# The last stage of a retention + two-MLP kernel, laid out by a table of offsets

## The chip, the cores and the metric

One core of a Trainium2 chip. The metric is the device time of one execution in microseconds (us); the kernel before is run three times and the median counts. A core has five engines with a queue each: TensorE (PE; its weight loads are PEld), VectorE (DVE), ScalarE (ACT), GpSimd (POOL) and SyncE (SP), which here issues the DMAs.

## What is computed

```
ret = scale * (q @ k.T) * Dmat          # 4 x 8 heads, 576 positions, decay per head
x   = (ret @ v) as (2304 tokens, 512)
h   = x @ w_in                          # 512 -> 2048
x2  = (h * clip(h + 3, 0, 6) / 6) @ w_out          # 2048 -> 512
h2  = x2 @ w2_in                        # 512 -> 1024
e   = exp(h2 - max(h2)); sm = e / (sum(e) + 1e-9); solu = h2 * sm
ln  = (solu - mean) / sqrt(var + 1e-6) * g_ln
out = ln @ w2_out                       # 1024 -> 512
```

All of it in fp32: each operand is split into a high and a low word (fp32r), and a product is three matmuls (high x high, high x low, low x high).

## The kernel before, in words

Tokens come in blocks of 512, 512, 512, 512 and 256 (numbers 0 to 4). Retention feeds the first MLP; part B of that MLP (the last ten of its sixteen d_ff tiles, `FB`) runs over the blocks in the order 3, 0, 1, 2, 4 and leaves x2 in DRAM (`x2f`). Part C is the second MLP. It works on pairs of token tiles (2 x 128 tokens), nine pairs, in the block order 2, 3, 0, 1, 4. The last stage is part B of block 4 and part C together, from about 440 us on.

For a pair i of part C:
- `load_x2` brings x2 from DRAM, `forms_x2` (L670) makes sums and differences of its quarters on GpSimd and splits them (L240 on ScalarE, L241 on GpSimd). x2 @ w2_in is done as a 2 x 2 block product with seven products instead of eight (`PRODUCTS`).
- `mm_h2` (L709): seven products of six matmuls, each in a PSUM bank of its own; ScalarE and VectorE add the banks up into u2, u4 and the two rows of h2, with a running maximum (L715, L730 to L741).
- `norm` (L746), for each row r of 128 tokens: exp (L750, ScalarE), h times e (L751, VectorE), square (L756, ScalarE), a few 128 x 1 steps, a power (L760 to L762, GpSimd), normalisation (L764, VectorE).
- `transpose` (L774): the 32-bit result is copied into two 16-bit halves (L780) and each goes through a DMA transpose issued by SP (L781). `split_turned` (L783) puts the halves together again (L771 ScalarE, L772 VectorE) and splits into lt (L240, L241).
- `mm_out` (L793): o of one tile, eight d_ff steps of three matmuls (L802), then a copy (L808) and a store.

`part_c` (L811) writes the order as a generator: four products, then the previous pair's `split_turned`, the next pair's load and forms, an o tile, the other products, the norms and transposes, another o tile; two o tiles and a remainder are left for the end. Only the loads marked in program order keep their place. All other instructions are put in order on each engine by a planner with its own estimates, which is how o, products and x2 matmuls come to alternate in small runs. Part B of block 4 runs by `mlp_by_ff` (L310): for each d_ff tile the h matmuls, and three tiles later its x2 matmuls, while the w2 weights come in one by one (`w2_load`, L604) and part C's first products run beside its end.

The PSUM banks: four single ones (`mm_tile`: h, x2, o) and two pairs of banks (`ps_c`, tag h2: accumulators of block 4's x2, then the products).

Of the kernel before, what the change touches and what calls it, by code (L numbers as in the profile page):

```python
# [21 lines left out]
NP = DM // 128  # L22
# [26 lines left out]
W2_FORMS = tuple(w for _, w in PRODUCTS)  # L49
LN_EPS = 1e-6  # L50
# [10 lines left out]

@with_exitstack
def retention_hardswish_solu_kernel(ctx, tc, kt, qt, kn, vt, w1, w2i, w2o, gln, decay, place, out):
# [3 lines left out]
    ve, se, ge = nc.vector, nc.scalar, nc.gpsimd  # L67
# [175 lines left out]
    def mlp_h(t, ff, g, slot):  # L243
# [18 lines left out]
        pool, tag, bufs = slot(ff)  # L262
        g[ff] = pool.tile([128, 2, n], F32R, tag=tag, bufs=bufs, name=f"g{t}_{ff}")
# [321 lines left out]
    def load_x2p(t, k):  # L585
        n = BLOCKS[t][1]
        if k * 512 < NP * n:
# [3 lines left out]
            nc.sync.dma_start(out=part, in_=x2s[t][:, k * share:(k + 1) * share])  # L591
# [3 lines left out]
    def evac_full(t, d, xp):  # L595
# [6 lines left out]
        nc.sync.dma_start(out=x2f[t][:, d], in_=e)  # L602

    def w2_load(f, home):  # L604
        for i in range(2):
            if home == "x4":
                w = [p0.tile([128, 2, 256], F32R, tag="x4", bufs=NP, name=f"w2{f}_{i}_{a}") for a in range(2)]
                w2t[f, i] = [a.rearrange("p a n -> p (a n)") for a in w]
                for a in range(2):
                    nc.sync.dma_start(out=f32(w2t[f, i][a]), in_=w2s[f, i][:, a])  # L610
            else:
                w = w_half(home, i, f"w2{f}_{i}")
                w2t[f, i] = [w[:, a] for a in range(2)]
                nc.sync.dma_start(out=f32(w), in_=w2s[f, i])
# [299 lines left out]
```

## Time and profile before

| | us |
|---|---|
| median of three executions (lowest, highest) | 707.6 (705.43, 711.11) |
| the profiled execution: its own time | 709.63 |
| its span, first to last instruction | 707.5 |
| TensorE busy in the span | 667.5 (94%) |
| VectorE, ScalarE, GpSimd busy | 324.7, 358.2, 315.5 |
| mean granted TensorE clock | 0.983 of 2.4 GHz |

The profiled execution is one execution: its span is what the rows measure, and its own time has what lies around the span. Busy time of TensorE counts pipelined matmuls, so that a busy share near 100% says only that it never stood still.

### The profile page before, as it was taken

What the parts mean: (1) busy time and instruction counts of PE and PEld (TensorE: products, weight loads), DVE (VectorE), ACT (ScalarE), POOL (GpSimd) and SP (SyncE); (2) the same over time, 40 slices, a digit from 0 to 9 for tenths busy, and PEclk for the clock granted to TensorE, in tenths of its full rate; (3) what the DMA queues carried; (4) which work ended last, traced back from release to release, by engine and by line L of the source; (5) the groups of instructions that cost most, each with busy time, mean ns of one, the idle gap of its engine ahead of it and who ended that gap; (6) DMA issues with size and microseconds to landing.
All of it is one profiled execution on the core that took longest, in us unless ns stands there. A gap on an engine that the chain in (4) does not pass through costs nothing.

```text
span 707.5 us, 10683 instructions
## 1 busy us (share of the span) xinstructions
PE 667.5 (94%) x3914; PEld 547.9 (77%) x3914; DVE 324.7 (46%) x606; ACT 358.2 (51%) x651; POOL 315.5 (45%) x342
## 2 busy tenths in 40 slices
PE   9999999999999999999999999985899888899967
PEld 6788888878889888888888888973667667777756
DVE  2555535163206351444743541115756666566660
ACT  6788746265427561553642640523535644555352
POOL 5676733023404241360430430756658756854242
PEclk9999999999999999999999999999899999899998
DMA  9989534295043525678547324994441344033531
GB/s 327 301 286 323 199 105 177 68 302 212 0 143 97 159 79 172 186 246 303 194 155 249 103 112 126 356 334 143 89 104 55 90 110 71 34 76 89 90 74 45
DMA packets 80296, 112.92 MB, mean 160 GB/s; under 512 B 42738, under 2 KB 48114, under 8 KB 80244
## 3 DMA queue, kind: packets, MB, share of 16 engines
q1 hardware_dynamic: 80096, 112.22, 50.6%
q8 instruction: 31, 0.51, 0.3%
q14 instruction: 21, 0.17, 0.1%
q10 hardware_dynamic: 148, 0.01, 0.0%
HBM read 70.80 MB, written 31.98 MB: 145 GB/s over the span
## 4 chain that ended last, share of the span: by engine, by line
PE 70%; POOL 7%; DVE 7%; DMA 6%; issue 6%; ACT 3%; SPq 0%; ACTq 0%; POOLq 0%; DVEq 0%
PE h L250 25%; PE x L271 17%; PE acc L271 9%; PE o L802 7%; PE h L724 5%; PE xp L373 3%; DMA lhT<-lh 3%; PE s L373 2%; POOL s L680 2%; POOL lt L241 2%; DVE h L751 2%; PE u L373 1%; DMA wraw<-in_w_dram 1%; DVE lh L780 1%; DMA rq<-in_qt_dram 1%
## 5 line engine op out<-in xcount | busy, mean ns | idle before, releaser
L265 POOL TENSOR_TENSOR g<-gf,g 128x512 fp32r<-128x512 f32 (+1 forms) x80 | 97.3, 1217 | 208.9 <-ACT g L264 197.6
L271 PE MATMUL x<-g,w 128*128 128x512 f32 x576 | 132.5, 389 | 0.5 <-DVE gf L261 0.4
L250 PE MATMUL h<-xb,w 128*128 128x512 f32 (+1 forms) x600 | 132.8, 359 | 0.1
L271 PEld LDWEIGHTS x<-g,w 128*128 128x128 f32 x576 | 108.0, 188 | 23.7 <-DVE gf L261 0.8
L802 PE MATMUL o<-w,lt 128*128 128x512 f32 (+1 forms) x456 | 109.0, 391 | 7.5 <-ACT lt L240 7.3
L261 DVE SCALAR_TENSOR_TENSOR gf<-r,h 128x512 f32<-128x512 f32 (+1 forms) x80 | 50.5, 632 | 139.7 <-ACT r L260 110.3
L250 PEld LDWEIGHTS h<-xb,w 128*128 128x128 f32 x600 | 100.1, 189 | 16.1 <-ACT x2p L346 0.5
L802 PEld LDWEIGHTS o<-w,lt 128*128 128x128 f32 x456 | 84.9, 195 | 28.0 <-ACT lt L240 9.4
L250 PE MATMUL h<-xB,w 128*128 128x512 f32 x360 | 82.4, 389 | 0.0
L271 PE MATMUL acc<-g,w 128*128 128x512 f32 (+1 forms) x384 | 79.9, 336 | 0.0
L250 PEld LDWEIGHTS h<-xB,w 128*128 128x128 f32 x360 | 67.6, 188 | 14.0
L260 ACT ACTIVATE r<-h,half 128x512 f32<-128x512 f32 (+1 forms) x80 | 50.9, 638 | 52.0 <-PE h L250 52.0
L271 PEld LDWEIGHTS acc<-g,w 128*128 128x128 f32 x384 | 63.3, 189 | 9.1
L264 ACT ACTIVATE g<-gf 128x512 fp32r<-128x512 f32 (+1 forms) x80 | 46.9, 586 | 44.8 <-DVE gf L261 43.2
L241 POOL TENSOR_TENSOR lt<-lT,lt 128x512 fp32r<-128x512 f32 x36 | 52.5, 1481 | 31.2 <-ACT lt L240 31.1
L724 PE MATMUL h<-w2t,xs 128*128 128x512 f32 x162 | 43.5, 407 | 9.7 <-DVE u L734 6.6
L131 DVE TENSOR_SCALAR wz<-wz 128x512 int32<-128x512 int32 x44 | 28.6, 650 | 40.1 <-ACT wz L123 40.0
L724 PEld LDWEIGHTS h<-w2t,xs 128*128 128x128 f32 x162 | 30.5, 195 | 19.2 <-DVE u L734 9.4
L771 ACT ACTIVATE lT<-lhT 128x1024 uint16<-128x1024 uint16 x18 | 24.6, 1368 | 36.2 <-DMA lhT<-lh 36.0
L123 ACT ACTIVATE wz<-wraw 128x512 f32<-128x512 f32 x44 | 29.0, 659 | 17.7 <-DMA wraw<-in_w2o_dram 8.9
L241 POOL TENSOR_TENSOR xb<-xa,xb 128x512 fp32r<-128x512 f32 (+7 forms) x32 | 27.5, 879 | 22.9 <-ACT xb L240 22.9
L715 DVE CUSTOM_DVE_ANT_0 h<-h,u 128x512 f32<-128x512 f32 x36 | 24.7, 685 | 25.1 <-PE h L724 18.3
(119 smaller groups left out, 863.5 us busy)
## 6 DMA issues: line engine op xcount, KB each, us to landing
wraw<-in_w_dram SPq DMA_DIRECT2D x32, 512.0 KB, 4.8
xs<-xb SPq DMA_DIRECT2D x12, 512.0 KB, 5.7
xB<-xs SPq DMA_DIRECT2D x12, 512.0 KB, 6.6
rv<-in_vt_dram SPq DMA_DIRECT2D x16, 288.0 KB, 5.3
x2l<-x2s SPq DMA_DIRECT2D x18, 256.0 KB, 4.2
out_dram<-osb SPq DMA_DIRECT2D x17, 256.0 KB, 2.1
x2s<-x2p SPq DMA_DIRECT2D x16, 256.0 KB, 2.7
x2f<-x2o SPq DMA_DIRECT2D x16, 256.0 KB, 3.6
```

Source lines behind the costliest of these rows:

```text
L123: first = se.activation(out=z.bitcast(F32), in_=raw[:, :, 1].bitcast(F32), func=ACTF.Prelu, scale=2.0 ** -112, alpha=2.0 ** 32)
L131: ve.tensor_scalar(out=z, in0=z, scalar1=3, scalar2=None, op0=ALU.logical_shift_left)
L241: ge.tensor_tensor(out=x[:, 1, c], in0=src, in1=f32(x[:, 0, c]), op=ALU.subtract)
L250: nc.tensor.matmul(hp, w1t[ff, 0][:, a, c], xb[t, p][:, b, :n], start=(p == 0 and i == 0), stop=(p == NP - 1 and i == 2),)
L260: se.activation(out=r, in_=hp, func=ACTF.Relu, scale=1.0 / 6.0, bias=half)
L261: ve.scalar_tensor_tensor(out=gf, in0=r, scalar=1.0, in1=hp, op0=ALU.min, op1=ALU.mult)
L264: se.activation(out=g[ff][:, 0], in_=gf, func=ACTF.Copy)
L265: ge.tensor_tensor(out=g[ff][:, 1], in0=gf, in1=f32(g[ff][:, 0]), op=ALU.subtract)
L271: nc.tensor.matmul(acc, w1t[ff, 1][:, a, c], g[:, b], start=(first and i == 0), stop=(last and i == 2))
L373: keep(nc.tensor.matmul(*args, **kw))
L724: nc.tensor.matmul(acc, x2w[i][x][k][a], w2t[w, k][b], start=(k == 0 and n == 0), stop=(k == 1 and n == 2),)
L802: nc.tensor.matmul(op, lt[:, a, ff % 4], w[b][:, c0:c0 + n], start=(ff == 0 and j == 0), stop=(ff == NFF2 - 1 and j == 2),)
```

## The change

Only the last stage is changed. Every instruction of it, on each of the five queues, is now kept in program order (`Pinned`), and the program order comes from a list of (time, step) pairs, sorted. The times are offsets in microseconds from the planned ends of the seven products of each pair, e[0] to e[6]; only their order is used. What the table lays out:

- Block 4's h for all ten d_ff tiles comes first (`mlp_hs`, still ordered by the planner), with its g kept in SBUF; its x2 follows as 40 units of three matmuls, by d_ff tile, in two single banks.
- The products run in groups of two, two, two and one (`GROUPS`), each group of two in one pair of banks. Between the groups stand fillers: five units of x2 in pair 0, four in pair 1, four units of o (three matmuls each) in pairs 2 to 7, none in pair 8. The rest of o follows.
- u2 and u4 live in the halves of row 1's h2, the weights of t4 in the tags r and gf, x2 in one load of 512 KB in other tags, the split forms in eight fixed tiles.
- `half_out`, `half_in`, `split_hi` and `split_lo` are the old `transpose` and `split_turned` in single steps, placed one by one.
- `STEPS_B` gets an entry of its own for each block.

The diff, cut to its core:

```diff
-STEPS_B = (6, 20, 42, 50, 58, 66)
+STEPS_B = ((6, 20, 42, 50, 58, 66), (6, 20, 42, 50, 58, 66), (6, 20, 42, 50))
-C_AHEAD = 8
+GROUPS = ((0, 1), (2, 3), (4, 5), (6,))
+UNIT, SMALL = 0.68, 0.36
+class Pinned:
+    def __init__(self, tc, engine):
+        self.keep, self.engine = tc.keep_in_program_order, engine
+    def __getattr__(self, name):
+        op = getattr(self.engine, name)
+        return lambda *args, **kw: self.keep(op(*args, **kw))
...
-        return pb.tile([128, 2, 512], F32R, tag="wb", bufs=8, name=name)
+        return pb.tile([128, 2, 512], F32R, tag="wbi" if i == 0 else "wbo", bufs=4, name=name)
...
-            x2r[i] = [p0.tile([128, 2, 256], F32, tag=tag, bufs=2, name=f"x2r{i}_{tag}") for tag in ("r", "gf")]
-        for k in range(2):
-            nc.sync.dma_start(out=x2r[i][k], in_=x2f[t][:, 2 * k:2 * k + 2, 256 * c:256 * c + 256])
+            raw = raw_bufs[i % 2]
+        x2r[i] = raw[:, :2], raw[:, 2:]
+        sy.dma_start(out=raw, in_=x2f[t][:, :, 256 * c:256 * c + 256])
...
+    def product(i, p):
+        if p % 2 == 0:
+            ab = ps_c.tile([128, 2, 512], F32, tag="h2", bufs=2, name=f"h2_{i}_{p}")
+            banks[i, p], banks[i, p + 1] = ab[:, 0], ab[:, 1]
...
-    def part_c():
...
+    load_x2(0)
+    load_x2(1)
...
+    to_load = {18: ("b11", "wbi"), 22: ("b21", "wbi"), 28: ("t2", "wi"), 36: ("t1", "wi")}
+    for i, _ in enumerate(mlp_hs(t, FB, g4, g_4)):
+        if i == 6:
+            for step in chain(*forms_x2(0)):
+                step()
+        if i in to_load:
+            w2_load(*to_load[i])
+    ve, se, ge, te, sy = (Pinned(tc, e) for e in (ve, se, ge, te, sy))
+    for f, home in (("b22", "wi"), ("t3", "x4"), ("t4", "r")):
+        w2_load(f, home)
...
+    fill(4, 0)
+    for i in range(last + 1):
+        starts.append(now)
+        for group in GROUPS:
+            for p in group:
+                at(now, product, i, p)
+                now += 2 * UNIT
+                ends[i, p] = now
+            fill(5 if i == 0 else 4, 4 if 2 <= i < last else 0)
+    fill(0, out_left)
...
+    for i in range(last + 1):
+        e = [ends[i, p] for p in range(7)]
+        for when, fn, *args in (
+            (e[0] + 0.2, first_u), (e[1] + 0.6, total, 0, 0, 2, 1), (e[2] + 0.1, add_u, 2, 2),
+            (e[3] + 0.1, add_u, 4, 3), (e[4] + 0.1, total, 0, 1, 4, 4), (e[4] + 0.8, top, 0), (e[4] + 1.0, exp, 0),
+            (e[5] + 0.1, total, 1, 1, 4, 5), (e[5] + 0.8, add_u, 2, 5), (e[4] + 2.9, weigh, 0),
+            (e[4] + 4.4, small, 0), (e[4] + 4.5, square, 0), (e[4] + 5.8, power, 0),
+            (e[6] + 0.1, total, 1, 0, 2, 6), (e[6] + 0.8, top, 1), (e[6] + 1.0, exp, 1),
+            (e[4] + 7.1, norm, 0), (e[6] + 2.4, weigh, 1), (e[6] + 4.0, small, 1), (e[6] + 4.0, square, 1),
+            (e[4] + 9.2, half_out, 0, 0), (e[4] + 9.9, half_out, 0, 1),
+            (e[6] + 5.3, power, 1), (e[6] + 6.7, norm, 1), (e[6] + 7.6, half_out, 1, 0), (e[6] + 8.3, half_out, 1, 1),
+            (e[4] + 15.3, half_in, 0, 0), (e[4] + 15.4, half_in, 0, 1),
+            (e[4] + 16.8, split_hi, 0, 0), (e[4] + 17.4, split_hi, 0, 1),
+            (e[4] + 17.5, split_lo, 0, 0), (e[4] + 18.8, split_lo, 0, 1),
+            (e[6] + 14.0, half_in, 1, 0), (e[6] + 14.1, half_in, 1, 1),
+            (e[6] + 23.5, split_hi, 1, 0), (e[6] + 24.1, split_hi, 1, 1),
+            (e[6] + 24.2, split_lo, 1, 0), (e[6] + 25.5, split_lo, 1, 1),
+        ):
+            at(when, fn, i, *args)
+        if i + 2 <= last:
+            at(starts[i] + 13.0, load_x2, i + 2)
+        if i < last:
+            spread(i + 1, starts[i], (0.0, 0.8, 3.6, 4.4, 3.6, 4.2, 4.8, 5.5, 5.2, 6.0, 7.3, 8.6))
+    for _, _, fn, args in sorted(events, key=lambda v: v[:2]):
+        fn(*args)
```

## Rows read from the trace of the kernel before

**Rows 1.** The page: busy time of TensorE, and its busy tenths in 40 slices.

```profile
PE 667.5 (94%) x3914; PEld 547.9 (77%) x3914; DVE 324.7 (46%) x606; ACT 358.2 (51%) x651; POOL 315.5 (45%) x342
PE   9999999999999999999999999985899888899967
```

**Rows 2.** Stretches: length, busy PE, PEld, DVE, ACT, POOL (instructions), PEclk, DMA, GB/s.

```profile
440.75:473.80 33.05, 33.05 (x259) 32.08 (x257) 4.90 (x11) 12.34 (x27) 21.01 (x25) 1.00 0.90 326
...
473.80:507.40 33.60, 19.95 (x63) 14.46 (x63) 20.79 (x43) 12.09 (x21) 19.13 (x22) 0.85 0.55 165
...
524.10:548.30 24.20, 23.19 (x96) 17.63 (x96) 15.76 (x33) 12.87 (x22) 16.72 (x18) 1.00 0.41 95
...
524.10:621.00 96.90, 87.49 (x353) 67.27 (x354) 61.49 (x127) 51.12 (x84) 66.20 (x72) 0.96 0.36 82
...
673.80:707.50 33.70, 24.65 (x119) 20.20 (x117) 11.48 (x24) 13.07 (x21) 10.45 (x13) 0.90 0.26 63
```

**Rows 3.** Chain of waits, 400 to 707.5: start, us, what.

```profile
413.71 27.20 PE x L271 x120
...
440.91 5.51 PE h L250 x46
...
603.71 2.93 PE h L724 x6
...
655.13 1.36 PE h L724 x6
...
691.30 12.88 PE o L802 x70
```

**Rows 4.** TensorE's waits, 415 to 707.5: total us, times, longest.

```profile
PE o L802 <- ACT lt L240: 7.3, 3, 5.6
PE h L724 <- DVE u L734: 6.6, 4, 3.5
PE h L724 <- DVE x2o L599: 4.4, 1, 4.4
...
PE h L724 <- DVE u L736: 3.1, 4, 0.8
```

**Rows 5.** Start of the stage: a stretch, GpSimd and VectorE in time, a load.

```profile
450.00:460.00 10.00, 10.00 (x85) 10.00 (x84) 1.26 (x3) 5.37 (x13) 9.92 (x12) 1.00 1.03 413
...
449.46 1.44 POOL L680 TENSOR_TENSOR s<-x2r 128x256 f32<-128x256 f32 x2 [1.87 <-DMA x2r<-x2f]
...
456.31 0.42 DVE L261 SCALAR_TENSOR_TENSOR gf<-r,h 128x256 f32<-128x256 f32 x1 [4.59 <-POOL xs L241]
...
x2r_gf<-x2f SPq DMA_DIRECT2D x3, 256.0 KB, 7.0
```

**Rows 6.** Lines from 520 to 690: duration ns min/median/max, first and last start.

```profile
L751 DVE SCALAR_TENSOR_TENSOR h<-h,e x14: 1208/2056/2294, 535.5 to 679.5; 128x1024 f32<-128x1024 f32 x14
...
L764 DVE TENSOR_SCALAR e<-h,stat x16: 808/812/1362, 520.2 to 683.8; 128x1024 f32<-128x1024 f32 x16
...
L715 DVE CUSTOM_DVE_ANT_0 h<-h,u x28: 664/690/693, 523.4 to 675.3; 128x512 f32<-128x512 f32 x28
...
L772 DVE COPY lT<-lhT x16: 741/748/1845, 528.2 to 689.2; 128x1024 uint16<-128x1024 uint16 x16
...
L750 ACT ACTIVATE e<-h,stat x14: 1135/1144/1160, 534.2 to 678.2; 128x1024 f32<-128x1024 f32 x14
...
L241 POOL TENSOR_TENSOR lt<-lT,lt x29: 1267/1297/2279, 530.9 to 690.0; 128x512 fp32r<-128x512 f32 x29
...
L680 POOL TENSOR_TENSOR s<-x2r_r x4: 730/738/747, 541.3 to 614.1; 128x256 f32<-128x256 f32 x4
...
L762 POOL TENSOR_TENSOR stat<-stat,mhalf x16: 541/732/1377, 519.6 to 682.7; 128x1 f32<-128x1 f32 x16
```

**Rows 7.** Transposes of lhT, 510 to 700: issue on SP (ns), landing.

```profile
L781 SPq DMA_TRANSPOSE lhT<-lh x32: 1237/1288/1397, 522.9 to 687.2; - x32
...
DMA to landing us min/median/max: 3.1/3.3/4.5
```

More of the change, by code (lines that the diff above doesn't have):

```diff
@@ L270, in mlp_x2 @@
         for i, (a, b) in enumerate(((0, 0), (1, 0), (0, 1))):
-            nc.tensor.matmul(acc, w1t[ff, 1][:, a, c], g[:, b], start=(first and i == 0), stop=(last and i == 2))
+            te.matmul(acc, w1t[ff, 1][:, a, c], g[:, b], start=(first and i == 0), stop=(last and i == 2))
     def mlp_hs(t, ffs, g, slot, keep_x=False):
@@ L746, in norm @@
-    def norm(i, r):
-        h, st = h2[i][r], stats[i][r]
+        return sums, his, los
+    def product(i, p):
+        if p % 2 == 0:
+            ab = ps_c.tile([128, 2, 512], F32, tag="h2", bufs=2, name=f"h2_{i}_{p}")
+            banks[i, p], banks[i, p + 1] = ab[:, 0], ab[:, 1]
+        x, w = PRODUCTS[p]
+        for k in range(2):
+            for n, (a, b) in enumerate(((0, 0), (0, 1), (1, 0))):
+                te.matmul(
+                    banks[i, p], x2w[i][x][k][a], w2t[w, k][b], start=(k == 0 and n == 0), stop=(k == 1 and n == 2),
+                )
@@ new lines, in row, with total @@
+    def row(i, r):
+        if (i, r) not in h2:
+            h2[i, r] = p0.tile([128, 2, 512], F32, tag="g", bufs=FA, name=f"h2_{i}_{r}")
+            stats[i, r] = pb.tile([128, 16], F32, tag="stat", bufs=6, name=f"stat{i}_{r}")
+        return h2[i, r], stats[i, r]
+    def total(i, r, m, u, p):
+        h, st = row(i, r)
+        ve.tensor_tensor_reduce(
+            out=h[:, m], in0=banks[i, p], in1=us[i, u], scale=1.0, scalar=MIN, op0=ALU.add, op1=ALU.max,
+            accum_out=st[:, m:m + 1],
+        )
@@ L793, in mm_out @@
     def mm_out(i):
-        r = tiles[i]
         n = DM // 2 if i == len(tiles) - 1 else DM
@@ new lines, in retention_hardswish_solu_kernel, with at, fill @@
+    events = []
+    def at(when, fn, *args):
+        events.append((when, len(events), fn, args))
+    now = 0.0
+    x2_4 = x2_units()
+    outs = chain(*(mm_out(i) for i in range(len(tiles))))
+    small_left, out_left = NP * len(FB), NFF2 * len(tiles) + NFF2
+    starts, ends = [], {}
+    def fill(n_small, n_out):
+        nonlocal now, small_left, out_left
+        for gen, n, length in ((x2_4, min(n_small, small_left), SMALL), (outs, min(n_out, out_left), UNIT)):
+            for _ in range(n):
+                at(now, next, gen, None)
+                now += length
+        small_left -= min(n_small, small_left)
+        out_left -= min(n_out, out_left)
@@ new lines, in retention_hardswish_solu_kernel, with spread, step @@
+    fill(4, 0)
[8 more added lines that the diff above has]
+    fill(0, out_left)
+    def spread(i, n, offsets):
+        made = {}
+        for k, offset in enumerate(offsets):
+            def step(k=k):
+                if not made:
+                    made[0] = list(chain(*forms_x2(i)))
+                made[0][k]()
+            at(n + offset, step)
```

270 lines of the change are left out of this document (124 added, 146 removed).

## The prediction

> **What bounds the kernel now.** I read the page first: TensorE has work in 94% of the span, and its slices are full up to about 475 us and ragged from there on [rows 1]. The reader should see that the ragged part is the last stage, the only one the change lays out anew. The table of stretches puts numbers on it [rows 2]: from 440.75 to 473.8 TensorE is always busy; from 473.8 to 507.4 it has 20 us of work in 33.6, at a mean granted clock of 0.85; then four repeats in 96.9 us, one per pair of token tiles, the first of 24.2; and from 673.8, the end of the last product, to the end of the span 24.7 of 33.7.
>
> How much of it is work? The chain of waits shows the pace: 120 matmuls of 512 columns in 27.20 us, or 0.2267 each, and 46 of 256 columns in 5.51, or 0.1198 each [rows 3]. By the loops the stage has, for the last block, 120 h and 120 x2 matmuls of 256 columns (28.75 us); 9 pairs x 7 products x 6 matmuls = 378 (85.7); and 18 o tiles x 24, of which the last is cut in halves: 408 of 512 columns (92.5) and 48 of 256 (5.75). In sum 212.7 us. It took from 440.75 to 704.2, where the last o ends (691.30 + 12.88), so 263.4. **50.7 us are loss.** TensorE's waits list 32.0 of them in seven rows, from 7.3 to 3.1 [rows 4]: 7.3 on lt, and 24.7 in the other six on something of VectorE or ScalarE that frees a PSUM bank (u, stat, x2o). The other 19 are the pipeline that drains and fills around each stop, and stretches at half of the 2.4 GHz: six matmuls in 2.93 us against 1.36 [rows 3]. From the clocks of [rows 2], 19.95 x 0.15 + 87.5 x 0.04 + 24.65 x 0.10, that is about 9 us.
>
> No other engine is full. Over the four repeats VectorE is busy 61.5 of 96.9 us, ScalarE 51.1, GpSimd 66.2 [rows 2], so 15.4, 12.8 and 16.6 us for a pair. A pair of TensorE alone (42 products, 48 o matmuls) is 90 x 0.2267 = 20.4.
>
> **The change, part by part.** *Arithmetic:* no matmul is added or removed. Per pair the vector work is the same list: seven bank evacuations, two rows of softmax and normalisation, four copies and four transposes out, four copies in, splits. x2 comes by one 512 KB load instead of two of 256 KB. I put these at nothing. The third entry of STEPS_B loses two steps that have nothing left to do (6 + 6 + 4 = 16, the number of halves), and the two names for the "wb" tiles split one pool of 8 into 4 + 4: nothing.
>
> *Last block's h first:* 120 x 0.1198 = 14.4 us, so to 455.15; then 4 x2 units (0.36 each) to 456.6. What has to be there then: xb and weights are resident, b11 may load as soon as two h's are done. All transfers up to the third x2 load are about 10.8 MB (six 1 MB forms and one more, one w_out form, 1.8 MB of x2 in and out); at 326 GB/s, the mean of this stretch before [rows 2], 33 us from 442.5 or to 475; at the 413 GB/s of its best ten microseconds [rows 5], to 468.7. The order is that of use, and the last form (t4) is wanted at 470, by which 9.2 MB are wanted, 22 to 28 us after 442.5: 465 to 471. So transfers are nearly hidden. GpSimd is tighter: the forms of pair 0 start when x2 lands (449.46 before, and the store that it waits for doesn't move) and are about 7.6 us of work beside one g split per h; before, gf on VectorE waits for GpSimd's xs there [rows 5]. With h's packed closer, two gf buffers and four banks let TensorE run six h's ahead; I take **3 us** of stall here, from 0 (all in time) to 8 (all of GpSimd's 7.6 first).
>
> *Products in groups of two, filler between:* two banks each, and the banks of a group are asked for again only a filler, a group and a filler later: 8.2 us with o between, 5.6 with x2 units. The releases (0.7 each) come 1 to 3 us after the group by the table. This is what takes away the 24.7 us on u, stat and x2o. By the table pair 0 lasts 9.52 + 20 x 0.36 = 16.7, pair 1 15.3, pairs 2 to 7 9.52 + 16 x 0.68 = 20.4 each, pair 8 9.52, and what is left of o 33.0 (40 units of 0.68 and 16 of 0.36): 456.6 + 16.7 + 15.3 + 122.4 + 9.5 + 33.0 = 653.5, and 3.3 for the last eviction and store as now (704.2 to 707.5): **a floor of 656.8.**
>
> *Everything pinned:* each engine now stands in the table's order, and behind a late instruction all of that engine waits. So I walked one middle pair with the rows' durations. VectorE's loop goes from the total of product 4 to the same of the next pair [rows 6]: total 0.77 with its read-out, top 0.21, exp on ScalarE 1.33 with its read-out, weigh 1.2 to 2.1 and 0.2, square 1.33, power on GpSimd 1.1 (0.73 and two small ones), norm 0.81, weigh of row 1 2.1 and 0.2: 9.2 to 10.1. Then row 1: two copies and row 1's small steps 1.7 (beside square on ScalarE), the next total 1.2 later behind first_u, norm 0.8, a copy 0.7, so 4.4; its transposes, issued at 1.29 each, land 3.3 us (3.1 to 4.5) after [rows 7], and half_in takes 0.75: 8.4 to 9.6. With 0.1 for each of ten hand-overs the loop is 18.6 to 20.7 us, and up to 21.5 where half_in on ScalarE (1.4) delays the next exp, against TensorE's 20.4. So it is about as long as what should cover it: queued behind half_in on VectorE are the next pair's totals, and TensorE waits for these only when they are 5 us late. Pair 0 and 1, with short fillers, give about 4 us of that lateness away (a loop of 19 to 20 in pair 1, of 15.3). o has more room: lt of pair i is ready 11 us ahead of its use by the table. I take **3 us** for the six pairs (0 if the loop is 19 to 20; 6 x 1.1 = 7 at 21.5).
>
> *The end:* pair 8 has nothing between its groups; the copy that frees the first bank pair comes behind row 1 of pair 7, and I take **1 us** (0 to 2). Row 1's lt must be there 27.2 us after the last product; before, the first split of the last pair was there at 691.3, 17.5 us after it [rows 3], but now there are two osb's and the transposes of pair 7 ahead of it: **2 us** (0 to 5). SP's queue: four transposes, two stores and a load a pair, about 6.5 of 20.4 us. Half clock after such stops: **1**.
>
> Two engines get denser. weigh takes 1.21 us at the least and 2.06 in the middle, GpSimd's split of lt 1.27 at the least and 2.28 at the most [rows 6]. The terms above have the contended value for one weigh in two.
>
> The Trainium skill (SBUF — State Buffer, section SBUF: two separate sides) says that VectorE operations with two SBUF inputs, or in a two-port mode, and GpSimd operations hold one shared port in turn, each for the whole instruction. The stretched values of both engines agree with that [rows 6]; what it would make of this change is the first rival.
>
> **Rivals.** *A. The port or the loop becomes the bound.* From the least values [rows 6], GpSimd needs 7 x 1.27 + 0.73 + 4 x 0.73 + 2 x 0.9 = 14.3 us a pair by itself (splits, xa, sums, power); weigh, norm and half_in of two rows (2.4 + 1.6 + 1.5), if each shuts it out, make 19.8 of 20.4, where it is 19.8 of 24.2 now. For: the stretched rows. Against: total is never stretched (0.66 to 0.69), and the table leaves GpSimd without work for 5 us a pair while weigh of row 0 runs. If only 88% of a period can be filled, it is 22.6, 2.2 x 6 pairs = 13 us more than the floor less 1 us of room: 667 + 12 = **679**.
>
> *B. The start stays late.* The forms, the x2 loads and row 0's first trip meet at 456 to 490, and pairs 0 and 1 have only 14.4 us of x2 to fill with. For: 7.0 us for a 256 KB load in this stretch [rows 5]. Price: x2 of pair 2 six us late, and lt of pair 0 (4 us of room) five late: 667 + 11 = **678**.
>
> *C. Slower: the fixed order ties the engines into one chain.* VectorE stands at half_in of row 1 until its transposes land, and the next pair's totals with it. If the way from half_out to half_in were 12 us instead of 4 to 5 (transposes behind 512 KB loads on the queues), the loop would be 28 us: 8 x 7.6 - 4 = 57 above the floor, so **714**; it decides from a period of 27.2 on, 6.8 above 20.4. Against: the longest landing seen is 4.5 us [rows 7].
>
> *D. No change:* the planner already placed o between products, and what it lost is not order but latency. Against: [rows 4] names banks, which the groups relieve. About **705**.
>
> **The numbers.** 656.8 + 3 + 3 + 1 + 2 + 1 = 666.8 of span. The profiled execution has 2.1 us beside its span and lies 2.0 above the median, so **667**. Chances: this forecast 0.62 (its own range, from the terms' ends, 657 to 680, the sum of the upper ends being 23), A 0.22, B 0.09, C 0.04, D 0.03. The range of 657 to 683 takes in A and B with some of their spread. About 1% is what a measurement of this kernel can tell. Faster by over 1%: 0.94; within 1%: 0.03; slower: 0.03.
>
> **What would show it.** Right: TensorE's waits after 440 fall from 32 to about 8; repeats of 20.4 to 21 us from 490 to 610; clock 1.00 there; last product near 628. Start: a TensorE gap near 455 on gf or x2 forms. A: repeats of 22 to 23 with waits on totals, GpSimd's splits near 1.7 on the mean. C: repeats above 27, VectorE waiting for transposes. Wrong if TensorE runs without gaps and still ends after 680, or if stages before 440 move.

## The result, and the profile after

| | before | after |
|---|---|---|
| median (lowest to highest), us | 709.36 (705.43 to 711.22) | 678.45 (677.07 to 678.76) |
| ratio, 95% interval | | 0.9568 (0.9519 to 0.9616) |
| profiled execution, its span | 709.63, 707.5 | 678.33, 676.5 |
| granted clock, mean | 0.983 | 0.995 |

The kernel became 31 us faster. 667 was predicted, with 657 to 683 around it: the direction and its cause were right, and the forecast was 11 us too low. Of these, 9.7 us lie in the span. The other 1.7 come from the step from span to time: the median of before was taken to lie 2.0 us below its profiled execution, but with a fourth execution (711.22) it lies 0.3 below, and the changed kernel's median lies at its profiled execution. All instructions that the table places have one line in the new profile, L69 (that of `Pinned`), so its rows are read by tile. L260, L271 and L283 are the old L250, L261 and L271.

TensorE's waits from 415 us on, the view of [rows 4] (us in total, times, longest):

```profile
PE h L69 <- DVE stat L69: 4.4, 1, 4.4
PE h L69 <- DVE h L69: 2.9, 5, 1.0
PE o L69 <- DMA w<-w2s: 1.6, 2, 1.2
PE h L260 <- DVE gf L271: 1.0, 1, 1.0
PE x L69 <- DVE gf L271: 0.9, 1, 0.9
```

10.8 us in five rows instead of 32.0 in seven. The stage by stretches, columns as in [rows 2]: h and block 4's first x2 up to the first product; pair 2; pair 6; pair 8; what is left of o, and the end.

```profile
442.13:460.34 18.21, 16.34 (x133) 15.93 (x132) 4.49 (x10) 9.31 (x23) 11.63 (x15) 1.00 0.89 332
492.50:515.09 22.59, 21.00 (x92) 16.75 (x91) 19.80 (x36) 13.35 (x21) 20.93 (x20) 1.00 0.75 195
579.85:601.37 21.52, 20.99 (x91) 16.73 (x90) 19.22 (x32) 12.88 (x21) 18.64 (x19) 1.00 0.43 105
622.91:639.89 16.98, 12.55 (x44) 9.66 (x42) 13.15 (x28) 6.99 (x11) 6.31 (x9) 0.80 0.38 78
639.89:676.50 36.61, 33.13 (x169) 28.23 (x167) 13.53 (x26) 16.33 (x26) 14.56 (x14) 1.00 0.28 73
```

The span that was predicted is 666.8, the measured one 676.5. The difference, term by term:

| part | predicted | measured | difference |
|---|---|---|---|
| stage begins (first h) | 440.75 | 442.13 | +1.4 |
| first h to first product: 15.85 of work, and stall | 3 | 2.36 | -0.6 |
| pairs 0 and 1 | 32.0 | 32.2 | +0.2 |
| pairs 2 to 7, 122.4 of work, and stall | 3 | 8.0 | +5.0 |
| pair 8, 9.52 of work, and stall | 1 | 7.5 | +6.5 |
| rest of o, 33.0 of work, and stall | 2 | 0.1 | -1.9 |
| half clock after stops | 1 | counted in pair 8 | -1.0 |
| last eviction and store | 3.3 | 3.5 | +0.2 |

Two terms carry it: the middle pairs and pair 8. The 1.4 us ahead of the stage are hardly work of the change: up to there TensorE and VectorE have the same instructions in the same order, the other engines differ only by one x2 form and two DMA issues from 434.9 us on, and the first h of the runs below lies anywhere from 439.6 to 443.0. They are therefore compared from the first product on; in the changed kernel it is 216.2 us from there to the end of the span (460.34 to 676.5).

**Pair 8.** TensorE in time, and the total that frees the banks on VectorE (start, us, what, in brackets the wait before it):

```profile
622.91 2.89 PE L69 MATMUL h<-w2b,xt 128*128 128x512 f32 x12
625.63 2.92 PE L69 MATMUL h<-w2t,xt 128*128 128x512 f32 x12
632.99 2.93 PE L69 MATMUL h<-w2b,xt 128*128 128x512 f32 x6 [4.43 <-DVE stat L69]
635.71 4.34 PE L69 MATMUL h<-w2t,xt 128*128 128x512 f32 x12
639.89 2.45 PE L69 MATMUL o<-w,lt 128*128 128x512 f32 x10
...
632.25 0.68 DVE L69 CUSTOM_DVE_ANT_0 h<-h,h 128x512 f32<-128x512 f32 x1
```

Two groups run, and the third wants banks that the first total of this pair still holds. Then six matmuls take 2.93 us and twelve 4.34, against 1.36 [rows 3] and 2.72. That is another 3.2 us, lost to the clock: the granted clock is 0.80 on the mean of this pair, with its stop of 4.43 us, and 1.00 in the pairs ahead of it.

**The middle pairs.** From pair 3 on TensorE stops for no more than 1.0 us at a time, and yet a pair lasts 21.5, not 20.4. So I follow one turn of the vector engines' loop, from one `weigh` of row 0 to the next (start, us, what):

```profile
579.14 2.31 DVE L69 SCALAR_TENSOR_TENSOR h<-h,e 128x1024 f32<-128x1024 f32 x1 [0.39 <-ACT e L69]
...
583.98 1.22 DVE L69 TENSOR_SCALAR e<-h,stat 128x1024 f32<-128x1024 f32 x1 [1.35 <-POOL stat L69]
...
585.12 1.76 DVE L69 SCALAR_TENSOR_TENSOR h<-h,e 128x1024 f32<-128x1024 f32 x1
585.76 3.97 POOL L69 TENSOR_TENSOR lt<-lT,lt 128x512 fp32r<-128x512 f32 x2
...
586.99 1.59 DVE L69 COPY lh<-e 128x1024 uint16<-128x1024 uint16 x1
587.17 1.15 ACT L69 ACTIVATE e<-h,stat 128x1024 f32<-128x1024 f32 x1 [1.53 <-DVE stat L69]
...
588.62 1.66 DVE L69 COPY lh<-e 128x1024 uint16<-128x1024 uint16 x1
...
589.69 0.91 POOL L69 TENSOR_TENSOR stat<-stat 128x1 f32<-128x1 f32 x2
...
591.26 1.22 DVE L69 TENSOR_SCALAR e<-h,stat 128x1024 f32<-128x1024 f32 x1 [0.38 <-POOL stat L69]
...
595.30 1.25 DVE L69 COPY lT<-lhT 128x1024 uint16<-128x1024 uint16 x1
...
596.66 1.15 ACT L69 ACTIVATE lt<-lT 128x512 fp32r<-128x512 f32 x2 [1.65 <-DVE lT L69]
...
598.15 0.67 DVE L69 CUSTOM_DVE_ANT_0 h<-h,h 128x512 f32<-128x512 f32 x1
...
599.43 1.15 ACT L69 ACTIVATE e<-h,stat 128x1024 f32<-128x1024 f32 x1
...
600.70 2.28 DVE L69 SCALAR_TENSOR_TENSOR h<-h,e 128x1024 f32<-128x1024 f32 x1 [0.40 <-ACT e L69]
```

Read it as one chain over three engines that each keep their order. `weigh` of row 0 (579.14), its square on ScalarE, its power on GpSimd, norm (583.98), `weigh` of row 1 (585.12), its square (ready at 588.4). Row 1's power should come now, but GpSimd is in two splits of lt until 589.69. So norm of row 1 comes at 591.26, then two copies, half_in (595.30), and ScalarE's split that waits for it; behind that stand half_in of row 1 and the next exp (599.43), and behind that the next `weigh`: 21.56 us after the last one.

Some of this chain is stretched. VectorE's forms from 536.77 to 622.91, after (busy us, mean ns | idle before):

```profile
L69 DVE COPY lh<-e 128x1024 uint16<-128x1024 uint16 x16 | 22.0, 1395 | 0.1
...
L69 DVE CUSTOM_DVE_ANT_0 h<-h,h 128x512 f32<-128x512 f32 x16 | 10.9, 678 | 0.0
L69 DVE COPY lT<-lhT 128x1024 uint16<-128x1024 uint16 x8 | 9.9, 1242 | 0.0
L69 DVE TENSOR_SCALAR e<-h,stat 128x1024 f32<-128x1024 f32 x8 | 9.8, 1221 | 6.9 <-POOL stat L69 6.9
```

and the same copy before, over four pairs:

```profile
L780 DVE COPY lh<-e 128x1024 uint16<-128x1024 uint16 x18 | 11.6, 689 | 0.1
```

The copy out takes 1.40 us instead of 0.69, half_in 1.24 and norm 1.22 where [rows 6] have medians of 0.75 and 0.81; the total is not stretched (0.68). VectorE is busy 19.2 of 21.5 us where it was 15.4 a pair. So both are in the chain: VectorE itself waits only 0.38 us for row 1's power (591.26), since its stretched copies fill nearly all of that time.

### The profile page after: what moved, and what is told of

It is laid out like the page before. It is cut to its first block, busy times and chain, and to the rows that moved or that the text cites. A ratio compares the mean times of both kernels' runs of the same rounds, so it can differ in the third digit from the quotient of the medians.

```text
span 676.5 us, 10633 instructions
## 1 busy us (share of the span) xinstructions
PE 657.2 (97%) x3914; PEld 545.0 (81%) x3914; DVE 350.2 (52%) x606; ACT 357.2 (53%) x651; POOL 329.8 (49%) x342
## 4 chain that ended last, share of the span: by engine, by line
PE 65%; DVE 10%; POOL 7%; DMA 7%; ACT 6%; issue 4%; SPq 0%; ACTq 0%; POOLq 0%; DVEq 0%
PE h L260 25%; PE x L283 17%; PE acc L283 8%; PE o L69 5%; PE h L69 3%; DVE h L69 3%; PE xp L385 3%; POOL lt L69 2%; DVE lh L69 2%; ACT e L69 2%; DMA wraw<-in_w_dram 2%; POOL stat L69 2%; PE s L385 1%; PE x L69 1%; DVE e L69 1%
## 5 line engine op out<-in xcount | busy, mean ns | idle before, releaser
L283 PE MATMUL x<-g,w 128*128 128x512 f32 x576 | 132.4, 389 | 0.1
L260 PE MATMUL h<-xb,w 128*128 128x512 f32 (+1 forms) x600 | 129.5, 359 | 1.0 <-DVE gf L271 1.0
L283 PEld LDWEIGHTS x<-g,w 128*128 128x128 f32 x576 | 108.0, 188 | 23.3 <-POOL g L277 0.5
L271 DVE SCALAR_TENSOR_TENSOR gf<-r,h 128x512 f32<-128x512 f32 (+1 forms) x80 | 50.6, 633 | 130.9 <-ACT r L270 105.5
L260 PEld LDWEIGHTS h<-xb,w 128*128 128x128 f32 x600 | 98.6, 189 | 17.1 <-DVE gf L271 1.2
L69 PE MATMUL o<-w,lt 128*128 128x512 f32 (+1 forms) x456 | 102.9, 378 | 1.6 <-DMA w<-w2s 1.6
L69 PEld LDWEIGHTS o<-w,lt 128*128 128x128 f32 x456 | 82.3, 188 | 18.4 <-DMA w<-w2s 2.4
L260 PE MATMUL h<-xB,w 128*128 128x512 f32 x360 | 82.4, 389 | 0.0
L260 PEld LDWEIGHTS h<-xB,w 128*128 128x128 f32 x360 | 67.6, 188 | 14.0
L69 POOL TENSOR_TENSOR lt<-lT,lt 128x512 fp32r<-128x512 f32 x36 | 58.4, 1639 | 22.6 <-ACT lt L69 12.2
L69 ACT ACTIVATE e<-h,stat 128x1024 f32<-128x1024 f32 x36 | 41.2, 1145 | 39.4 <-DVE stat L69 39.4
L283 PE MATMUL acc<-g,w 128*128 128x512 f32 (+1 forms) x264 | 61.8, 360 | 0.0
L69 PE MATMUL h<-w2t,xt 128*128 128x512 f32 x216 | 55.5, 401 | 2.9 <-DVE h L69 2.9
L283 PEld LDWEIGHTS acc<-g,w 128*128 128x128 f32 x264 | 46.9, 188 | 8.7
L69 PEld LDWEIGHTS h<-w2t,xt 128*128 128x128 f32 x216 | 41.0, 193 | 13.6 <-DVE h L69 5.0
L69 PE MATMUL h<-w2b,xt 128*128 128x512 f32 x162 | 41.7, 403 | 4.6 <-DVE stat L69 4.4
L69 DVE COPY lh<-e 128x1024 uint16<-128x1024 uint16 x36 | 42.8, 1211 | 0.2
L69 PEld LDWEIGHTS h<-w2b,xt 128*128 128x128 f32 x162 | 30.5, 193 | 12.7 <-DVE stat L69 6.7
```

Source lines behind the costliest of these rows:

```text
L69: return lambda *args, **kw: self.keep(op(*args, **kw))
L260: nc.tensor.matmul(hp, w1t[ff, 0][:, a, c], xb[t, p][:, b, :n], start=(p == 0 and i == 0), stop=(p == NP - 1 and i == 2),)
L271: ve.scalar_tensor_tensor(out=gf, in0=r, scalar=1.0, in1=hp, op0=ALU.min, op1=ALU.mult)
L283: te.matmul(acc, w1t[ff, 1][:, a, c], g[:, b], start=(first and i == 0), stop=(last and i == 2))
```

## The experiments

Four questions: which part of the change gave the 31 us; what holds pair 8; what sets 21.5; and whether the mended versions add up. Times without an interval are of one execution.

### What gave the gain: unpinned, x2_half, groups43

*unpinned*: everything else stays, but the engines are not pinned, so that the planner orders the new stage.

```diff
-    ve, se, ge, te, sy = (Pinned(tc, e) for e in (ve, se, ge, te, sy))
```

> The same list of steps in the same program order, but nothing of the last stage is kept in program order: the planner orders each engine by its own estimates. Theory 'the fixed order is part of the gain': the planner interleaves as before, TensorE's waits on banks come back to 10 us or more, span 685 to 700. Rival 'grouping, filler and program order are the gain and pinning adds little': span 673 to 680.

Measured 690.62 (span 688.6). TensorE's waits, same view and stretch as above:

```profile
PE h L733 <- DVE stat L745: 6.6, 3, 2.3
PE h L733 <- DVE h L756: 6.1, 3, 3.4
PE o L836 <- POOL lt L826: 3.7, 3, 2.1
PE o L836 <- ACT lt L821: 2.5, 2, 1.9
```

18.9 us of stops, 12.7 of them on the totals and additions that free banks. The span lies in the range of the theory, 685 to 700. Against 678.45 the fixed order is worth about 12 us; the rest of the change gives the other 18 or 19, even where the planner orders it. The parts of that rest were not all taken apart: the two runs that follow spoil the filler and the groups, one at a time.

*x2_half*: 16 of block 4's x2 units go ahead of the first product instead of between the products of pairs 0 and 1.

```diff
-    fill(4, 0)
+    fill(20, 0)
...
-            fill(5 if i == 0 else 4, 4 if 2 <= i < last else 0)
+            fill(3 if i == 0 else 2, 4 if 2 <= i < last else 0)
...
-            at(starts[i] + 13.0, load_x2, i + 2)
+            at(starts[i] + (11.0 if i == 1 else 13.0), load_x2, i + 2)
```

> Half of block 4's x2 units (20 of 40) run before the first product, so that pairs 0 and 1 have 12 and 8 units as filler instead of 20 and 16. Work is the same. Theory 'x2 is the cover of the first pairs' chains': what is missing, 7.2 us of cover, comes back as waits of products on banks and of the first o units on lt in pairs 0 to 3; the way from the first h to the start of pair 4 grows by 4 to 7 us, span 680 to 684. Rival 'lateness saturates anyway': the lateness that pairs 0 and 1 give away is lost at pair 8 only once, and the span is within 2 us of 676.5.

Measured 682.93 (span 681.2). From the first h to the end 239.4 us, against 234.4: of the 5.8 us of matmuls that were moved ahead (16 x 0.36; the 7.2 of the expectation counts 20 units), 5.0 are lost. The stops that come back, on TensorE:

```profile
495.50 4.40 PE L69 MATMUL h<-w2b,xt 128*128 128x512 f32 x12 [2.69 <-DVE h L69]
...
502.43 3.68 PE L69 MATMUL o<-w,lt 128*128 128x512 f32 x10 [1.88 <-POOL lt L69]
```

The middle pairs end at the same 21.53. So filler is worth nearly its own time here: the first `weigh` comes 32.5 us after the first h in the changed kernel and 37.2 here, so the vector loop starts 4.7 us later.

*groups43*: groups of four and three products with fillers twice as long.

```diff
-GROUPS = ((0, 1), (2, 3), (4, 5), (6,))
+GROUPS = ((0, 1, 2, 3), (4, 5, 6))
...
-            fill(5 if i == 0 else 4, 4 if 2 <= i < last else 0)
+            fill(10 if i == 0 else 8, 8 if 2 <= i < last else 0)
```

> The products in groups of four and three with twice the filler behind each, instead of 2, 2, 2, 1. Same work. Theory 'the distance from a group to its next use of the banks is what took away the waits': the second group asks at once for the banks of products 0 to 2, and the next pair's first group for those of 4 to 6; before the second group there are 5.4 us of filler and none between the first two bank pairs, so waits on totals come back, 1 to 3 us a pair, span 683 to 700. Rival 'it is the amount of filler in a pair, wherever it stands': span 675 to 679.

Measured 684.27 (span 682.5, just under the theory's 683 and well above the rival's 679), 222.2 us from the first product: 6 more.

```profile
PE h L69 <- DVE stat L69: 12.2, 6, 5.0
```

The waits on the total's banks go from 4.4 us in one to 12.2 in six. That two banks and a filler lie between two uses is what holds TensorE free of VectorE, as the prediction had it.

### What holds pair 8: fill8

In pair 8 o units stand between the groups too, and row 1's last splits come 6 us earlier in the table.

```diff
-            fill(5 if i == 0 else 4, 4 if 2 <= i < last else 0)
+            fill(5 if i == 0 else 4, 4 if 2 <= i <= last else 0)
...
-            (e[6] + 23.5, split_hi, 1, 0), (e[6] + 24.1, split_hi, 1, 1),
-            (e[6] + 24.2, split_lo, 1, 0), (e[6] + 25.5, split_lo, 1, 1),
+            (e[6] + 23.5 - (6.0 if i == last else 0.0), split_hi, 1, 0), ...
```

> Pair 8 gets four o units behind each of its four groups too (and row 1's last splits stand 6 us earlier in the list, so that the shorter remainder of o finds them). Theory 'lateness comes due': VectorE is some 5 us late from pair 3 on; with o between groups the banks are asked for 8.2 us later and little of that shows, in pair 8 they are asked for at once and all of it shows (4.4 us of wait and a stretch at half clock, 17.0 us instead of 9.5). Then pair 8 lasts about 21.5, its wait falls below 1 us, the remainder of o lasts 22 us plus at most 2 of wait for the last lt, and the span is 669 to 672, the time 0.988 to 0.993 of the changed kernel's. Rival 'the end is a chain': what ends last is the way from the last product to the last lt, some 25 us; then o waits 5 us or more for lt in the remainder and the span stays at 675 to 678.

Measured 676.75 (673.28 to 677.35), ratio 0.9532 (0.9502 to 0.9562); in the profiled execution 213.1 us from the first product. The interval overlaps the changed kernel's (0.9519 to 0.9616): by the medians the time is 0.9975 of it, where 0.988 to 0.993 was expected. The profiled execution is the fastest of the four, and what follows is read from it alone. The stop of 4.43 is gone, but one comes that was not there, in the last row's o:

```profile
655.92 0.73 PE L69 MATMUL o<-w,lt 128*128 128x512 f32 x2 [2.20 <-ACT lt L69]
657.27 3.06 PE L69 MATMUL o<-w,lt 128*128 128x512 f32 x12 [0.62 <-POOL lt L69]
```

From the `weigh` of row 0 of pair 8 to the end are 30.1 us instead of 34.6, but that `weigh` stands 1.4 later after the first product (183.0 against 181.6): 3.1 of the 7.5 us come back in this execution, and 1.7 by the medians. The 1.4 come from pair 3, where nothing was edited: a stop of 1.79 us there is followed by matmuls at a granted clock of 0.76 (531 to 538), and the pair lasts 24.1 us instead of 21.7. The stop in pair 8 was a matter of bank room. What is left of o is now 10.9 us shorter, and o waits for the last row's lt. What the earlier splits alone do was not tried.

### What sets 21.5: act_out, skip_lo, power_first

*act_out*: the second of the two copies in `half_out` goes from VectorE to ScalarE.

```diff
-        ve.tensor_copy(out=part, in_=words[:, w])
+        if w:
+            se.activation(out=part, in_=words[:, w], func=ACTF.Copy)
+        else:
+            ve.tensor_copy(out=part, in_=words[:, w])
```

> The second of each row's two 16-bit copies out (half_out, w = 1) goes from VectorE to ScalarE. Theory 'VectorE is the bound, stretched by GpSimd' (busy 19.2 of a 21.5 us period): VectorE falls to about 16.5 us a pair, ScalarE rises from 12.9 to 15.6, the period falls to TensorE's 20.4 to 20.7, pair 8 loses 2 to 4 us of its stall, span 665 to 670. Rival 'a chain of hand-overs through four engines and the transposes is the loop, whoever does the copy': ScalarE's copy takes 1.37 on the same way, the period stays 21.3 to 21.7 and the span 675 to 678.

Measured 672.17 (671.5 to 673.24), ratio 0.9481 (0.9457 to 0.9504), an interval wholly below the changed kernel's; 209.4 us from the first product. VectorE is busy 15.9 of 21 us, GpSimd as before:

```profile
555.00:576.00 21.00, 20.94 (x93) 17.03 (x92) 15.93 (x33) 15.15 (x24) 18.12 (x19) 1.00 0.43 104
```

*skip_lo*: three of the four GpSimd splits of each x2 are left out from pair 2 on. The kernel leaves work out, so its time is a probe and not a gain.

```diff
-            lambda a=a, b=b, v=v: ge.tensor_tensor(...) for a, b, v in splits
+            lambda a=a, b=b, v=v: ge.tensor_tensor(...) for a, b, v in splits[:1 if i >= 2 else 4]
...
-                made[0][k]()
+                if k < len(made[0]):
+                    made[0][k]()
```

> Leaves work out: from pair 2 on the low words of three of the four split x2 forms are not computed (three 128 x 512 subtractions on GpSimd a pair; old values stay). Theory 'GpSimd stretches VectorE': GpSimd falls from 19.2 to some 14 us a pair, VectorE's copies out fall from 1.40 to 1.0 us or less and its busy time from 19.2 to 17 or less, the period to 20.4 to 20.7, span 664 to 669. Rival 'chain of hand-overs': the subtractions left out are not on the chain, so the period stays 21.3 to 21.7 and the span 674 to 678.

Measured 669.34 (span 667.6); 209.0 us. GpSimd is busy 14.0 us in a pair instead of 18.6, and VectorE still 18.35:

```profile
574.29:594.96 20.67, 20.67 (x92) 16.71 (x91) 18.35 (x32) 13.15 (x21) 14.02 (x15) 1.00 0.44 105
...
594.91 1.23 DVE L69 SCALAR_TENSOR_TENSOR h<-h,e 128x1024 f32<-128x1024 f32 x1
```

That the copies would become short was wrong: their mean stays at 1395 ns, and the two splits of lt that stand beside them are still there. `weigh` falls from 2.01 to 1.46: that of row 0, which has no split beside it any more, takes 1.23 us (594.91) and not 2.28.

*power_first*: only GpSimd's order changes. Row 1's two splits of lt go behind the next pair's power, and no instruction is added or removed.

```diff
-            (e[6] + 24.2, split_lo, 1, 0), (e[6] + 25.5, split_lo, 1, 1),
+            (e[6] + 26.2, split_lo, 1, 0), (e[6] + 26.9, split_lo, 1, 1),
```

> Only GpSimd's order changes: row 1's two splits of lt (3.5 to 4 us in the middle pairs, while weigh and the copies out of VectorE run) stand behind the power of the next row instead of ahead of it; no work is added or removed. Theory 'the two engines stretch each other where the table sets them side by side': weigh of row 1 (1.76) and the copies of row 0 (1.6 each) come down, power of row 1 no longer waits behind a split, VectorE's busy time falls from 19.2 to 18 or less, period 20.4 to 20.9, span 668 to 672. Rival 'total work of both engines on the port is what counts, wherever it stands': the splits collide with later VectorE work instead, period 21.3 to 21.8, span 675 to 678.

Measured 671.2 (span 669.4); 210.9 us. The same place of the loop as above, on all engines:

```profile
581.25 1.76 DVE L69 SCALAR_TENSOR_TENSOR h<-h,e 128x1024 f32<-128x1024 f32 x1
...
583.13 0.68 DVE L69 COPY lh<-e 128x1024 uint16<-128x1024 uint16 x1
...
583.85 0.68 DVE L69 COPY lh<-e 128x1024 uint16<-128x1024 uint16 x1
584.01 0.87 POOL L69 TENSOR_TENSOR stat<-stat 128x1 f32<-128x1 f32 x2 [2.08 <-DVE stat L69]
...
585.68 1.64 DVE L69 TENSOR_SCALAR e<-h,stat 128x1024 f32<-128x1024 f32 x1
587.36 2.81 DVE L69 COPY lh<-e 128x1024 uint16<-128x1024 uint16 x2
...
590.80 0.63 ACT L69 ACTIVATE xt<-s 128x512 fp32r<-128x512 f32 x1 [4.42 <-POOL s L69]
...
595.50 1.14 ACT L69 ACTIVATE e<-h,stat 128x1024 f32<-128x1024 f32 x1
```

While GpSimd waits, the copies of row 0 take 0.68 us instead of 1.59 and 1.66. Norm of row 1 follows 4.4 us after the `weigh` above (585.68) instead of 6.1. Part of the stretch only moves on, as the rival had it: with the splits behind the power, norm of row 1 takes 1.64 us instead of 1.22, and row 1's two copies take 2.81 instead of 2.26.

TensorE's pairs 3 to 7 last 20.40 us, which I first read as a loop that fits. It doesn't. The starts of row 0's `weigh` give the loop itself, and its distance from the start of the pair's products shows how late the vector engines run:

| | loop, pairs 4 to 7 | TensorE's pairs 2, 3, 4, 5, 6, 7 | `weigh` of row 0 after the pair's start, pairs 3 to 7 |
|---|---|---|---|
| changed kernel | 21.51, 21.56, 21.50 | 22.59, 21.68, 21.59, 21.49, 21.52, 21.54 | 21.4, 20.9, 20.8, 20.9, 20.8 |
| act_out | 20.74, 20.80, 21.31 | 22.45, 20.48, 20.72, 20.73, 20.72, 21.96 | 21.2, 21.2, 21.3, 21.3, 21.9 |
| skip_lo | 20.69, 20.70, 20.70 | 22.37, 20.40, 20.40, 20.40, 20.67, 20.69 | 19.7, 20.0, 20.3, 20.6, 20.7 |
| power_first | 21.03, 21.04, 21.04 | 24.64, 20.40, 20.40, 20.40, 20.40, 20.45 | 17.5, 19.0, 19.6, 20.3, 20.9 |

In power_first the loop is 21.04. TensorE can run at 20.40 only because it stopped for 4.2 us in pair 2 (24.64), which let the vector engines catch up; they then fall behind by 0.64 a pair. All three edits shorten the loop, by 0.5 to 0.8 us (but for act_out's last turn, 21.31), and none brings it to 20.4: with a quarter less work on GpSimd or a sixth less on VectorE it is 20.7 or more. What remains in power_first is again a queue: ScalarE's xt waits 4.42 us for a sum on GpSimd (590.80), and half_in, a split and the next exp stand behind it.

### Do they add up: both, pf_fill8, pf_fill8_load, pf_fill8_load_act, mix

*both* is fill8 and act_out together, their two diffs unchanged.

> The o filler in pair 8 and ScalarE's share of the copies out together. Alone they took 3.1 us (filler) and 6.8 us (copies) off the way from the first product to the end of the span (216.2 before either). If lateness and VectorE's load are the two causes and the second feeds the first, they overlap in pair 8: 205 to 208 us from the first product to the end, span 666 to 668, time 667 to 670. Rival 'with o moved into pair 8 the chain from the last product to the last lt sets the end': o waits 3 us or more in the remainder and the span is that of the copies alone, 669 to 671.

Measured 670.09 (668.86 to 672.68), ratio 0.9474 (0.9438 to 0.9509); 207.6 us, within the 205 to 208 that were expected. It beats the changed kernel by 8 us, with intervals that don't touch. Its median is the lowest of the kernels that do the whole computation, but its interval overlaps those of act_out, pf_fill8 and mix, so it can't be called faster than these. In the profiled executions, 1.8 of the 3.1 us of fill8 are added to act_out's 209.4.

*pf_fill8* is power_first and fill8 together; the splits of the last pair stand at +17.5, +18.1, +18.2 and +18.9.

> GpSimd's order (splits of row 1 behind the power of the next row) and o filler in pair 8 together. Theory 'two separate losses': the order gives the six pairs their 20.4 us (210.9 us from the first product to the end), the filler takes away the 3.5 us of bank wait that is left in pair 8; 206 to 208 us from the first product, periods 20.4, pair 8 20.4 to 20.9, span 664 to 667. Rival 'the tail is a chain': with o used up in pair 8, o waits 3 us or more for the last lt and 209 to 211 us remain.

Measured 672.42 (670.78 to 673.68), ratio 0.9495 (0.9472 to 0.9517); 210.0 us, where 206 to 208 were expected.

```profile
648.52 13.67 PE L69 MATMUL o<-w,lt 128*128 128x512 f32 x57 [3.49 <-POOL lt L69]
```

Pair 8 runs free, but pair 7's splits of lt now stand behind pair 8's powers. GpSimd itself waits 2.98 us there for row 1's statistics and starts those splits only at 647.20, and their o units wait 3.49.

*pf_fill8_load* also deals with a wait that I had not foreseen. In pair 2 of the changed kernel o waits 1.6 us for the last w_out tile. SP in time there:

```profile
494.98 3.20 SPq L69 DMA_DIRECT2D x2f<-x2o  x4
498.27 1.09 SPq L69 DMA_DIRECT2D w<-w2s  x2
```

The load (498.27) stands behind the stores of block 4's x2, and those behind the last x2 matmuls. Here it is issued ahead of the evictions:

```diff
-                if k == end and d % 2 == 1:
-                    for dd in (d - 1, d):
-                        evac_full(t, dd, accs[d // 2][:, dd % 2])
                 if d == NP - 1 and k % 2 == 1 and k != 3:
                     w2_load(max(0, k // 2 - 1), "wbo" if k == 1 else "wo")
+                if k == end and d == NP - 1:
+                    for dd in range(NP):
+                        evac_full(t, dd, accs[dd // 2][:, dd % 2])
```

> The same, and the load of the last w_out weights is issued ahead of the four x2 stores of block 4 instead of behind them (the stores wait for VectorE, and o waited 1.4 to 1.7 us for these weights in pair 2). Theory: the wait of o on w in pair 2 goes from 1.5 us to under 0.5 and the way from the first product to the end is 1 to 2 us shorter than in the run beside it. Rival: the transfer itself (contention in this stretch) is late, the wait stays at 1 us or more.

Measured 672.91 (670.56 to 673.4), ratio 0.9492 (0.9468 to 0.9517); 212.4 us. The expected gain of 1 to 2 us didn't come. The wait on w is gone, and the next units of o wait for lt instead:

```profile
512.32 4.21 PE L69 MATMUL o<-w,lt 128*128 128x512 f32 x9 [5.50 <-POOL lt L69]
```

*pf_fill8_load_act* adds act_out's edit to that.

> The same, and the second copy out of each row on ScalarE. Theory 'TensorE is the bound of the middle pairs once VectorE's period is under 20.4': no gain there, the periods stay 20.4; only the last chain (copies out beside each other) may gain up to 1 us. Rival 'VectorE's load still costs': 2 us or more off.

Measured 675.25 (674.93 to 678.15), ratio 0.9545 (0.9521 to 0.9569); 215.2 us: the four edits together can't be told from the changed kernel by their intervals. TensorE waits for GpSimd's lt 9.1 us in two stops, and the loop of pairs 4 to 7 is 22.69, 21.62 and 21.78, against 21.04 to 21.07 in pf_fill8_load: in this order the copy on ScalarE lengthens the loop that it shortened in act_out.

*mix* keeps power_first's order to pairs 1 to 6, and has fill8's filler.

```diff
-            (e[6] + 24.2, split_lo, 1, 0), (e[6] + 25.5, split_lo, 1, 1),
+            (e[6] + (18.2 if i == last else 24.2 + (2.0 if 0 < i < last - 1 else 0.0)), split_lo, 1, 0), ...
```

> GpSimd's order of the run before (splits of row 1 behind the next row's power) only for pairs 1 to 6; pairs 0 and 7 keep the table's, since there the later split made o wait 1.7 and 3.5 us for lt; o filler in pair 8 as before. Theory: periods of 20.4 to 20.6 without those two waits; 204.5 to 207 us from the first product to the end, span 664 to 667, time 665.5 to 668.5. Rival 'the last chain sets the end anyway': the wait returns in front of the last two o tiles and 209 us or more remain.

Measured 671.97 (670.8 to 673.83), ratio 0.9476 (0.9454 to 0.9498); 210.2 us in the profiled execution, the slowest of five, where 204.5 to 207 were expected. TensorE's pairs 2 to 7 are 22.10, 20.40, 20.57, 21.06, 21.03, 21.04, and the loop of pairs 4 to 7 is 21.04 each time, as in power_first. Pair 2's stop is 2.5 us shorter, so the vector engines run about 2 us later (`weigh` 19.6 us after the start of pair 3, not 17.5), and TensorE meets their pace two pairs on. The order that seemed to fit in power_first was the same 21.04 with more slack ahead of it.

## Why the prediction was right, and where it was off

The range holds the result, but the forecast's 667 is not what happened. 678.45 is nearly the price of rivals A (679) and B (678), and neither happened as it was told: about half of A's loss came in the middle pairs, and pair 8 made up the rest.

**Right: what was lost before.** 24.7 us on u, stat and x2o [rows 4] were said to be waits for PSUM banks, which groups of two with a filler take away. 7.3 are left, 4.4 of them in the one pair that has no filler. groups43 and x2_half bring them back by spoiling the group or the filler. The clock is 1.00 in the middle pairs, as was said. From the first h to the end of o it is now 230.9 us for 212.7 of work, a loss of 18 where it was 50.7.

**Right: the start.** 3 us of stall were taken between h and the first product; it is 2.4, in two waits on gf (1.0 and 0.9), and the engine named is behind them: VectorE's gf waits up to 2.7 us for GpSimd's splits of g, between which the x2 forms stand. Rival B is out: no product waits for an x2 load or a form.

**Off: the six pairs, 3 us taken, 8.0 measured.** The step was the loop of one pair, 18.6 to 20.7 and up to 21.5, from which I took half a microsecond a pair above 20.4. It is 21.5, the upper end, for which the prediction's own price was 7; pair 2's wait on a load, below, makes most of the eighth. That the walk's upper end is 21.5 too is partly chance. Its condition was half_in on ScalarE ahead of the next exp; it is there, but the exp (599.43) comes at most 0.4 us after its maximum (599.08). The time is lost in row 1: from its copies (586.99) to the next total (598.15) are 11.2 us, where the walk had 8.4 to 9.6 and a few hand-overs of 0.1. Two things were missing in the walk. The copies out went in at 0.7 and norm at 0.8, their values before, though GpSimd's order was about to move under them: they measure 1.40 and 1.22. And row 1's power stands behind two splits on GpSimd until 589.69, a hand-over that I had priced at 0.1.

Against A it was said that the table leaves GpSimd without work for 5 us a pair while `weigh` of row 0 runs: in pair 6 GpSimd is busy 18.6 of 21.5 us, and its splits of lt run beside that `weigh`, which takes 2.3. Rival A had named the cause, the stretch by GpSimd, and its sign was there (splits of lt at 1.67 us on the mean), but at half its price: 21.5 a pair and no long waits on totals, not 22.6. Its sum of 19.8 had left the copies out, and with them (4 x 0.68) it is 22.5, more than the turn that was measured.

That the loop and not TensorE sets the middle is shown by act_out, skip_lo, power_first and mix, in which the loop measures 20.7 to 21.3 and TensorE follows it as soon as its slack is used up. How much of the 21.5 is stretch and how much is order is shown in part. In skip_lo row 1's place is as it was, and what is gained at `weigh` of row 0 (2.28 to 1.23) is stretch alone. power_first changes both at once: it takes 1.7 us off row 1's place and only 0.5 off the loop.

**Off: pair 8, 1 us taken, 7.5 measured.** The prediction said that the loop's lateness is about 4 us after pairs 0 and 1, and that TensorE only waits for totals that are 5 us late. That room is a filler's, and pair 8 has none. With o between, the third group asks for its banks 10.9 us after the pair's start (four times 2.72); without it, after 5.4. The first total starts 9.3 us after the start (632.25): in time for the one and 4 us late for the other. The lateness was in the text, and was not charged where it counted. The wait of 4.43 and the 3.2 us at a lower clock after it make the 7.5. fill8 shows it: with filler in pair 8 the stop is gone.

**Off: a load on SP.** 1.6 us on the last w_out tile. I had counted SP's time per pair, but had not looked at what the load is queued behind. In pf_fill8_load the wait is gone and nothing is gained, since TensorE waits for lt a little later; what the earlier load would give in the changed kernel's own order was not tried.

**Off, to the good: the end.** 2 us were taken for the last row's lt, 0.1 was measured. GpSimd's last splits of it:

```profile
664.03 2.53 POOL L69 TENSOR_TENSOR lt<-lT,lt 128x512 fp32r<-128x512 f32 x2 [0.19 <-ACT lt L69]
```

They end 26.7 us after the last product, and the table had asked for them at 27.2, so they come just in time. fill8 takes 10.9 us of o out of that stretch and pays 2.8 us there: pair 8 and the end trade against each other. Whether the stop in pair 8 itself gave the last lt its time is not shown.

**Rivals C and D** are out: a pair takes 21.5 us and not 27 or more, and the time fell by 31.

## What to carry to other kernels

In a software pipeline on engines that keep their order, compute the loop from one step of the critical row to the same step of the next, through every queue that it passes, and compare it with the period; if it is longer, lateness grows until TensorE is held to the loop's pace, here from pair 3 on, and all of it shows where slack ends, here in the last pair. A period equal to TensorE's work in one experiment doesn't prove that the loop fits: measure the vector engines' own period and their distance from TensorE. And durations measured beside other neighbours are not constants: when the order of GpSimd changes, price VectorE's copies again.

## What the runs showed of the hardware

A reorder on one engine changed the durations on another: the copy of 128x1024 16-bit elements takes 0.68 us with GpSimd idle (power_first, 583.13) and 1.59 and 1.66 beside its splits (586.99, 588.62). In the changed kernel one `weigh`, two copies and two splits fill 585.12 to 590.28, 5.16 us; their least values add up to 1.21 + 2 x 0.68 + 2 x 1.27 = 5.11 [rows 6; the copy from power_first]. So in that place they took about as long as if they had run one after the other. The fit is not exact, since the end of a sum on GpSimd (to 585.79) and a few 128 x 1 steps lie in it too. And it can't hold of all that the two engines do: rival A's sum with the copies, 22.5, is more than the turns of 21.5 and 21.04.

The Trainium skill (SBUF — State Buffer, section SBUF: two separate sides) says that GpSimd and those VectorE operations that use the shared port hold it in turn, an instruction at a time, and the sum of that one place agrees. The total, which stands among them, is not stretched: 678 to 682 ns on the mean in the changed kernel, skip_lo and power_first, and 0.67 us at 598.15, beside GpSimd's splits of x2 (595.89 to 599.39).
